# Later batches: K to lhs by DMA transposes, chunk bounds by a VectorE tree

## The chip, the cores and the metric

The kernel runs on one core of a Trainium2 chip. Its engines are TensorE (PE, matmuls; PEld is its weight load), VectorE (DVE), ScalarE (ACT), GpSimd (POOL) and SyncE (SP, which here only issues DMAs; ACT and POOL issue some as well). Each engine works through its own queue in order, and they wait for one another by semaphores. The metric is the device time of one execution in microseconds; the time of a kernel is the median of its runs. Less is better.

## What is computed

Attention in which every query attends to at most six chunks of 32 keys, then a two-layer MLP with an ELU. Batch 4, 8 heads, 768 positions, head dimension 64; the MLP goes from 512 to 2048 and back to 512 over all 3072 tokens.

```python
k_chunks = k.reshape(B, H, nc, chunk, D)                 # chunk = 32, nc = 24
k_min = np.min(k_chunks, axis=3)
k_max = np.max(k_chunks, axis=3)
ub = np.sum(np.maximum(q[:, :, :, None, :] * k_min[:, :, None, :, :],
                       q[:, :, :, None, :] * k_max[:, :, None, :, :]), axis=-1)
ub = np.where(pos[:, None] // chunk >= np.arange(nc)[None, :], ub, -1e9)
top_chunks = np.argsort(ub, axis=-1)[..., -6:]
scores = scale * np.matmul(q, k.transpose(0, 1, 3, 2))
mask = sel & (pos[:, None] >= pos[None, :])              # sel: key's chunk is among the query's six
attn = softmax(np.where(mask, scores, -1e9))
x = np.matmul(attn, v)                                   # heads side by side: 3072 x 512
h = x @ w_in
out = np.where(h > 0, h, np.exp(np.minimum(h, 0)) - 1) @ w_out
```

## The kernel before

**Tiling.** The work is cut into nine blocks of query positions: three of 256 in batch 0 (blocks 0 to 2) and two of 384 in each of batches 1 to 3 (blocks 3 to 8). Heads go in four pairs, so that a pair's two head dimensions fill 128 partitions. Per block there is a front (K and Q are brought into shape, chunks are selected), an attention part for each pair, and the MLP.

**Front.** K, Q and V come in as f32 tiles of 128 positions by 8 heads by 64 (`kld`, `qld`, `vld`, issued at L442). `prep_k` turns one pair's K with PE transposes against an f32 identity (L484, one per 128 positions, into PSUM). From that PSUM tile VectorE takes the maximum and the minimum of every 32 columns with two `tensor_reduce` (L504) and their difference (L521); minimum and difference are the weights `kst` of the bounds. ACT casts the same PSUM tile to bf16. In blocks 0 and 1 (`DIRECT_K`) it writes the two heads straight into `lhs` (L511); in the others it writes one tile `kb` (L516), and two DMAs per pair copy its halves to rows 0 to 63 of `lhs` (L519). Rows 64 to 95 of `lhs` hold a constant, -40000 where a key's chunk is the row's number, written once at the start (L418, and L420 by DMA for the second set). `prep_q` does the same for Q: PE transposes, ACT copies to `QTf` in f32 (L534), two casts per pair to rows 0 to 63 of `rhs` (by ACT in blocks 0 and 1, L538; by POOL in the others, L542), and a rectified copy `Qrl` on VectorE (L545).

**Selection.** The bounds are matmuls of `kst` with `QTf` and `Qrl` (L563). VectorE transposes them in 32 x 32 blocks (L574), finds the sixth largest of each query (L581), compares (L585) and transposes the 0/1 rows back, straight into rows 64 to 95 of `rhs` in blocks 0 to 2 (L591), or into `msk` (L597), from which eight DMAs copy them (L601). So a score matmul over 96 rows (L625) adds -40000 where a chunk isn't selected.

**Attention and MLP.** ACT takes the exponential of the scores into `pt` (L641, L645), VectorE zeroes what lies above the diagonal (L652, L659), PE multiplies with V, which has a column of ones (L674; `vext`, cast by POOL at L475), VectorE divides (L683, L685), and the result is turned into `xt` by a DMA transpose on SP (L698), or on PE in the first and last block. The MLP computes 16 groups of four matmuls per block (L713), each followed by an exponential on ACT (L717), a subtraction of 1 on POOL (L719) and the gate product `gT` on VectorE (L721, 144 in the kernel), and then the second layer (L732), whose result goes out over ACT (L736) and SP (L739). The f32 weights are loaded and cast by DMAs that POOL issues (L459, L463).

**Order.** Nothing is scheduled by hand line by line. Every step is an `op` with an engine, an assumed duration, its reads and writes, and a priority: the block's slot, plus a value per kind of step, block and engine from the table `SHIFTS`. `Plan.run` plays the steps through with these durations and so fixes each engine's order when the kernel is built; on the chip each engine follows it. `CAPS` gives the number of buffers per kind. PE's gaps up to an assumed 70 us are filled with matmuls on a junk tile (L849).

Of the kernel before, what the change touches and what calls it, by code (L numbers as in the profile page):

```python
# [48 lines left out]
DIRECT_K = (0,1)  # L49
# [3 lines left out]
MASK_DVE = (0,1,2)  # L53
SW_LOADS = ("k1","q1","v0","v1","k2","q2","v2")
ACT_LOADS = ("k0", "q0")
SW_ORDER = ("k1","v0","q1","v1","wi0","wi1","wi2","wi3","k2","q2","v2","wo0","wo1","wo2","wo3")
QC_ACT = (0, 1)
VC_ACT = ()
# [5 lines left out]
CAPS = dict(psT=1, psS=2, psO=1, psM=4, kld=2, qld=2, vld=1, QTf=6, Qrl=6, kb=3, kmx=3, ubT=2, thr=2,  # L64
# [8 lines left out]
    ('cast', 'POOL'): (23.69201, -1.09103, 8.72813, 12.08469, 27.05452, 15.31053, -7.22527, 12.46238, -4.92564),  # L73
    ('gate', 'POOL'): (-15.60205, 0.0, 0.0, 0.0, 0.0, 0.0, 0.0, 0.0, 0.0),
    ('init', 'DVE'): (2.32119, 0.0, 0.0, 4.74909, 8.35134, 25.74829, 26.2034, 24.17884, 8.09583),
    ('init', 'POOL'): (-10.70374, 13.48214, 0.0, 0.0, 0.0, 0.0, 0.0, 0.0, 0.0),
    ('init', 'SP'): (0.0, 0.0, 5.0031, 0.0, 0.0, 0.0, 0.0, 0.0, 0.0),
    ('kld', 'ACT'): (7.73677, 0.0, 0.0, 0.0, 0.0, 0.0, 0.0, 0.0, 0.0),
    ('kld', 'SP'): (10.12848, 0.0, 0.0, 5.57881, -2.49779, -2.11959, 2.10101, -9.36615, 8.45298),
    ('kld', 'POOL'): (0.0, -10.22887, -28.22296, 0.0, 0.0, 0.0, 0.0, 0.0, 0.0),  # L80
    ('mlp_in', 'ACT'): (-5.95241, -10.04818, -17.00783, -25.26762, -14.11138, -10.95442, -15.33449, -28.79886, -25.74958),
    ('mlp_in', 'DVE'): (-17.75866, -10.06772, 0.30993, -42.84851, -12.09763, -12.58286, -21.31407, -27.98266, -20.97106),
    ('mlp_in', 'PE'): (16.73975, -0.43165, -16.68227, -9.61, 1.47816, -3.63864, -12.99075, 8.98426, -6.01021),
    ('mlp_in', 'POOL'): (14.0813, -3.42504, -7.07691, 9.34007, -3.88006, 14.95892, 2.46731, -3.39101, -20.64038),
    ('mlp_out', 'ACT'): (4.22, -1.17489, -2.72673, 1.20556, 3.98277, -5.60986, 4.9958, 11.5461, -16.3697),
    ('mlp_out', 'PE'): (21.15925, 11.91005, 16.97289, -0.35066, 1.28499, 10.01749, 2.87573, 19.97835, -0.98046),
    ('mlp_out', 'SP'): (1.98487, -6.20708, 4.90006, 5.76266, -7.76736, -15.54093, 15.2713, 2.49768, -7.95696),
    ('prep_k', 'ACT'): (-19.18919, -30.78931, -27.5262, -6.91647, -6.7488, -6.36581, -3.55271, -15.77301, -8.33444),
    ('prep_k', 'DVE'): (-28.28537, -41.41256, -18.41797, -26.42048, 4.76573, -40.62348, -18.36229, -14.34176, -9.12351),
    ('prep_k', 'PE'): (-12.63275, 2.81869, -6.61429, -24.32332, 11.32822, -0.45579, -0.25696, 3.77564, -5.23277),  # L90
    ('prep_k', 'SP'): (0.0, 0.0, -13.31443, -2.45234, -6.22613, 4.3603, -1.19146, 4.6153, 18.19868),
    ('prep_q', 'ACT'): (-33.9716, -32.60888, -11.98557, -31.52365, -6.14348, -38.53006, -19.34522, -0.18424, -32.21482),
    ('prep_q', 'DVE'): (-12.55718, -8.37218, -7.36189, -0.77956, -17.2022, -13.25357, -2.48719, 12.39928, 9.4983),
    ('prep_q', 'PE'): (-0.49879, -10.22351, -6.76805, -3.36762, 13.26419, -0.11343, -0.82527, 2.63172, 17.99147),
    ('prep_q', 'POOL'): (0.0, 0.0, -1.80424, 5.83533, 31.22304, -2.13268, 13.63839, 14.88967, 8.56983),
    ('qld', 'ACT'): (4.95999, 0.0, 0.0, 0.0, 0.0, 0.0, 0.0, 0.0, 0.0),
    ('qld', 'SP'): (1.83573, 0.0, 0.0, 15.2204, -34.93755, -8.03456, -21.48739, -7.26273, -2.89049),
    ('qld', 'POOL'): (0.0, 18.35032, 4.84342, 0.0, 0.0, 0.0, 0.0, 0.0, 0.0),
    ('score', 'ACT'): (-15.06279, 15.94173, -8.66685, 9.77749, -9.24225, 2.15661, -0.32595, 11.29037, -1.82453),
    ('score', 'DVE'): (-14.86996, -1.8364, -14.54096, -15.51319, -24.21821, -11.17075, -7.10068, 12.60874, -21.25837),  # L100
    ('score', 'PE'): (-32.41584, -3.52461, -7.04682, -18.09124, -31.88096, -7.62331, -8.80699, -3.45233, -3.08179),
    ('select', 'DVE'): (15.81252, 43.76081, 24.59488, 29.28494, 4.04565, 23.13038, 28.69119, 20.70793, 39.51627),
    ('select', 'PE'): (-27.57642, 1.02863, -33.96822, -11.24403, -50.42777, -17.9141, -33.86792, -39.9782, -44.24463),
    ('select', 'SP'): (0.0, 0.0, 0.0, -13.94033, -23.5977, -19.02693, 6.4407, -14.63791, -5.86023),
    ('vld', 'POOL'): (-4.26654, 3.53215, -20.45399, 0.0, 0.0, 0.0, 0.0, 0.0, 0.0),
    ('vld', 'SP'): (0.0, 0.0, 0.0, 11.82217, -6.42843, 0.45266, 3.43084, -5.00112, 20.242),
    ('w_in', 'POOL'): (-5.96518, 0.0, 0.0, 0.0, 0.0, 0.0, 0.0, 0.0, 0.0),
# [202 lines left out]
def kernel(  # L310
# [68 lines left out]
    def pool_op(occ, fn, writes=(), reads=()):  # L379
        return op("POOL", occ, 60, fn, reads=reads, writes=writes)  # L380
# [500 lines left out]
```

## Time and profile before

| | us |
|---|---|
| median of three runs | 296.47 (296.07 to 300.57) |
| the profiled execution's own time | 297.83 |
| its span, first to last instruction | 295.9 |
| PE, DVE, ACT, POOL busy | 277.3, 204.8, 196.4, 137.0 |
| mean granted TensorE clock | 0.965 |

The span is what the views below divide up; it is 1.9 us shorter than the execution's own time. An engine is busy while at least one of its instructions runs. Instructions of one engine overlap somewhat (the next starts while the last one drains), so a group's mean duration is more than the distance at which such instructions follow one another; for PE, which is pipelined, much more.

```profile
L719 POOL TENSOR_SCALAR e<-e 128x384 f32<-128x384 f32 (+1 forms) x144 | 69.8, 489 | 120.6 <-ACT e L717 60.0
L721 DVE SCALAR_TENSOR_TENSOR gT<-psM,e 128x384 bf16<-128x384 f32 (+1 forms) x144 | 71.8, 506 | 25.4 <-POOL e L719 24.0
L516 ACT ACTIVATE kb<-psT 128x384 bf16<-128x384 f32 (+1 forms) x28 | 13.7, 489 | 12.0 <-DVE kst L504 7.8
L504 DVE TENSOR_REDUCE kmx<-psT 128x12 f32<-128x384 f32 (+1 forms) x32 | 16.6, 519 | 6.7 <-PE psT L484 6.3
L475 POOL TENSOR_SCALAR vext<-vld 128x384 bf16<-128x384 f32 (+1 forms) x36 | 17.5, 509 | 5.7 <-DMA vld<-in_v_dram 3.0
...
lhs<-kb SPq DMA_DIRECT2D x48, 48.0 KB, 2.6
...
xt<-on SPq DMA_TRANSPOSE x28, 2.8
```

These are groups of the page's fifth and sixth part: line, engine, operation, output and inputs, count, busy time in us and mean ns of one, then the engine's idle time just before them and who ended most of it; for DMA issues, count, size and median us from issue to landing.

### The profile page before, as it was taken

The numbers are of one execution on the slowest core, as the hardware profiler recorded it, in microseconds if no ns is written. First come the engines' busy times: TensorE is split into PE (matmuls) and PEld (weight loads), VectorE is DVE, ScalarE is ACT, GpSimd is POOL, SyncE is SP. The second block draws the span as 40 slices with busy tenths as digits, with TensorE's granted clock in tenths as the row PEclk, the third lists the DMA queues.
The fourth block names the chain that finished last, engine by engine and source line by source line (L and its number), as shares of the span: only waits on it lengthen the run. The fifth ranks groups of instructions, "written<-read, shape, count | busy, mean of one in ns | idle before, by whom it ended". The sixth has DMA issues, their size and how long they took to land.

```text
span 295.9 us, 7293 instructions
## 1 busy us (share of the span) xinstructions
PE 277.3 (94%) x2544; PEld 179.4 (61%) x2544; DVE 204.8 (69%) x667; ACT 196.4 (66%) x458; POOL 137.0 (46%) x278
## 2 busy tenths in 40 slices
PE   8576879999999998999999999999999999999993
PEld 8354557569658655666565556766565456655541
DVE  8778698897768886855699966666678727634620
ACT  2795587299559528997397349995496389854621
POOL 7697674034915924845365414750285024404510
PEclk9865798999999999999999999999999999999999
DMA  8889998268936665968845662602210420010001
GB/s 189 221 149 214 273 198 149 65 174 180 208 66 180 150 135 122 243 158 205 199 95 153 144 175 68 153 16 85 74 44 17 82 94 2 0 39 35 38 35 72
DMA packets 86885, 36.23 MB, mean 122 GB/s; under 512 B 74176, under 2 KB 82880, under 8 KB 86848
## 3 DMA queue, kind: packets, MB, share of 16 engines
q1 hardware_dynamic: 79424, 27.38, 37.7%
q0 software_dynamic: 5344, 7.87, 13.0%
q10 hardware_dynamic: 2080, 0.52, 0.8%
q8 instruction: 20, 0.33, 0.5%
q14 instruction: 17, 0.14, 0.2%
HBM read 27.26 MB, written 6.29 MB: 113 GB/s over the span
## 4 chain that ended last, share of the span: by engine, by line
PE 73%; DVE 13%; ACT 6%; DMA 4%; issue 2%; POOL 1%; SPq 0%; POOLq 0%; DVEq 0%; ACTq 0%
PE psM L713 23%; PE psM L732 23%; PE psS L625 10%; PE o_bank L674 6%; PE psT L484 5%; DVE gT L721 3%; PE psT L563 2%; DMA rhs<-msk 2%; PE o_bank L849 2%; ACT rhs L538 2%; DVE rhs L591 2%; DVE kmx L504 2%; ACT lhs L511 1%; DMA kld<-in_k_dram 1%; DVE thr L581 1%
## 5 line engine op out<-in xcount | busy, mean ns | idle before, releaser
L719 POOL TENSOR_SCALAR e<-e 128x384 f32<-128x384 f32 (+1 forms) x144 | 69.8, 489 | 120.6 <-ACT e L717 60.0
L713 PE MATMUL psM<-xt,w_in_sb 128*128 128x384 bf16 (+1 forms) x576 | 109.0, 313 | 1.6 <-DVE gT L721 1.4
L732 PE MATMUL psM<-w_out_sb,gT 128*128 128x512 bf16 x384 | 99.1, 379 | 0.0
L641 ACT ACTIVATE pt<-psS 128x384 bf16<-128x384 f32 (+1 forms) x164 | 87.7, 568 | 13.2 <-PE psS L625 12.7
L721 DVE SCALAR_TENSOR_TENSOR gT<-psM,e 128x384 bf16<-128x384 f32 (+1 forms) x144 | 71.8, 506 | 25.4 <-POOL e L719 24.0
L717 ACT ACTIVATE e<-psM 128x384 f32<-128x384 f32 (+1 forms) x144 | 68.8, 486 | 21.9 <-PE psM L713 18.4
L713 PEld LDWEIGHTS <-w_in_sb 128*128 128x128 bf16 x576 | 55.4, 99 | 28.1 <-issue 2.4
L625 PE MATMUL psS<-rhs,lhs 96*128 96x384 bf16 (+2 forms) x304 | 66.3, 286 | 2.5 <-DMA rhs<-msk 1.5
L732 PEld LDWEIGHTS <-gT 128*128 128x128 bf16 x384 | 36.0, 98 | 31.5 <-issue 1.2
L625 PEld LDWEIGHTS <-lhs 96*128 96x128 bf16 x312 | 29.4, 100 | 19.4 <-issue 2.3
L542 POOL TENSOR_SCALAR rhs<-QTf 64x384 bf16<-64x384 f32 (+1 forms) x56 | 29.4, 526 | 14.4 <-ACT QTf L534 10.8
L736 ACT ACTIVATE osb<-psM 128x512 f32<-128x512 f32 x24 | 14.4, 600 | 30.5 <-PE psM L732 30.3
L674 PEld LDWEIGHTS <-pt 128*128 128x128 bf16 x672 | 27.8, 99 | 9.8 <-issue 1.7
L674 PE MATMUL o_bank<-vext,pt 128*128 128x65 bf16 x672 | 30.9, 195 | 0.8 <-DVE on L685 0.5
L652 DVE TENSOR_TENSOR pt<-pt,tri 128x512 bf16<-128x512 bf16 x36 | 17.0, 475 | 7.0 <-ACT pt L641 6.6
L516 ACT ACTIVATE kb<-psT 128x384 bf16<-128x384 f32 (+1 forms) x28 | 13.7, 489 | 12.0 <-DVE kst L504 7.8
L504 DVE TENSOR_REDUCE kmx<-psT 128x12 f32<-128x384 f32 (+1 forms) x32 | 16.6, 519 | 6.7 <-PE psT L484 6.3
L534 ACT ACTIVATE QTf<-psT 128x384 f32<-128x384 f32 (+1 forms) x32 | 15.9, 498 | 7.6 <-PE psT L484 7.6
L475 POOL TENSOR_SCALAR vext<-vld 128x384 bf16<-128x384 f32 (+1 forms) x36 | 17.5, 509 | 5.7 <-DMA vld<-in_v_dram 3.0
L685 DVE TENSOR_TENSOR on<-o_bank,rcp 128x384 bf16<-128x384 f32 (+1 forms) x36 | 18.2, 506 | 0.6
L484 PE MATMUL psT<-ident_f,kld 128*128 128x128 f32 x88 | 16.0, 285 | 1.3 <-ACT QTf L534 0.6
L484 PE MATMUL psT<-ident_f,qld 128*128 128x128 f32 x88 | 15.8, 285 | 1.4 <-ACT lhs L511 1.0
(69 smaller groups left out, 241.6 us busy)
## 6 DMA issues: line engine op xcount, KB each, us to landing
out_dram<-osb SPq DMA_DIRECT2D x24, 256.0 KB, 2.2
kld<-in_k_dram SPq DMA_DIRECT2D x19, 256.0 KB, 4.0
qld<-in_q_dram SPq DMA_DIRECT2D x19, 256.0 KB, 3.9
vld<-in_v_dram SPq DMA_DIRECT2D x18, 256.0 KB, 3.5
lhs<-kb SPq DMA_DIRECT2D x48, 48.0 KB, 2.6
w_in_sb<-in_moe_w_in_dram POOLq DMA_DIRECT2D x4, 512.0 KB, 9.5
w_out_sb<-in_moe_w_out_dram POOLq DMA_DIRECT2D x4, 512.0 KB, 11.9
vld<-in_v_dram POOLq DMA_DIRECT2D x6, 256.0 KB, 5.0
```

What stands on the lines that cost most here:

```text
L484: nc.tensor.transpose(ps.get()[:, P * n:P * (n + 1)], xb.get()[:, n, hs, :].rearrange("p h d -> p (h d)"), ident_f)
L504: nc.vector.tensor_reduce(out=out, in_=psk.get()[:, 0:w].rearrange("p (c w) -> p c w", w=CHUNK), axis=AX.X, op=o)
L542: pool_op(110 + pool_ns(w), lambda h=h: nc.gpsimd.tensor_scalar(out=rhs[RH[i]][0:64, h, j, 0:w], in0=qtf.get()[64 * h:64 * h + 64, 0:w], s ...
L625: nc.tensor.matmul(sps.get()[:, o + pc:o + pc + n], lhsT=lhs[s][0:96, hd, P * kb:P * (kb + 1)], rhs=rhs[y][0:96, hd, j, c0 - lo:c0 - lo + ...
L641: op("ACT", act_ns(wtot), 140, lambda pt=pt, sps=sps, hd=hd, wtot=wtot: nc.scalar.activation(out=pt.get()[:, hd, 0:wtot], in_=sps.get()[:, ...
L674: nc.tensor.matmul(o3.get()[:, hd, qi, :], lhsT=pt.get()[:, hd, P * qt + off:P * qt + off + P], rhs=vexts[s][:, kb, hd, :], start=(kb == 0 ...
L685: op("DVE", dve_ns(w), 140, lambda: nc.vector.tensor_tensor(out=on.get()[:, 0:nt, :, :].rearrange("p q h d -> p h q d"), in0=o3.get()[:, : ...
L713: op("PE", 1 + w / 2.4, 200, lambda fc=fc, kk=kk, h_ps=h_ps: nc.tensor.matmul(h_ps.get()[:, 0:w], lhsT=w_in_sb[:, kk, P * fc:P * (fc + 1)] ...
L717: op("ACT", act_ns(w), 200, lambda e=e, h_ps=h_ps: nc.scalar.activation(out=e.get()[:, 0:w], in_=h_ps.get()[:, 0:w], func=AF.Exp), reads=[ ...
L719: op("POOL", pool_ns(w), 72, lambda e=e: nc.gpsimd.tensor_scalar(out=e.get()[:, 0:w], in0=e.get()[:, 0:w], scalar1=-1.0, scalar2=1.0, op0= ...
L721: g_ops.append(op("DVE", dve_ns(w), 130, lambda e=e, h_ps=h_ps, fc=fc: nc.vector.scalar_tensor_tensor(out=gT[fc // 4].get()[:, fc % 4, 0:w ...
L732: op("PE", 216, 200, lambda tt=tt, fc=fc, o_ps=o_ps: nc.tensor.matmul(o_ps.get(), lhsT=gT[fc // 4].get()[:, fc % 4, P * tt:P * (tt + 1)], ...
```

## The change

Batch 0 (blocks 0 to 2) keeps the PE transposes of K and the reduces. For batches 1 to 3 `prep_k` is no longer called. Three new steps take its place. `load_kn` lets POOL issue DMAs that load K as bf16 into tiles `kn`, 128 positions by 8 heads by 128, of which the second 64 columns of each head are padding that holds the constant of rows 64 to 95 (filled once by `init_pads` and `init_kn`). `turn_k` issues on SP one DMA transpose per tile, which writes all eight heads' `lhs` columns of these 128 positions, constant rows included. `bounds_k`, once per batch, loads K a second time in f32, chunk by chunk: a partition is one chunk of one head (96 partitions for four heads), and the 32 positions lie along the row. VectorE halves the row pairwise with `tensor_tensor` maximum and minimum, 1024, 512, 256, 128 and 64 elements, twice (for four heads each); two PE transposes per batch and four small ACT copies put the results into `kst`.

The Q casts of blocks 0 and 1 move from ACT to VectorE (`QC`). Block 2's K goes to `lhs` directly instead of over `kb`. `kb` and the DMA copies from it are gone, as are those of the constant rows. `lhs` becomes two tensors by batch parity, `rhs` two instead of three; Q and V are buffered tile by tile, and a V cast takes all eight heads of 128 positions. The order of POOL's first DMAs, some assumed durations and all of `SHIFTS` are new, so every engine's order is another.

```diff
-DIRECT_K = (0,1)
-QC_ACT = (0, 1)
+QC = {0: "DVE", 1: "DVE"}
-SW_ORDER = ("k1","v0","q1","v1","wi0","wi1","wi2","wi3","k2","q2","v2","wo0","wo1","wo2","wo3")
+SW_ORDER = ("k1", "q1", "v0", "v1", "wi0", "wi1", "wi2", "wi3", "k2", "q2", "v2", "wo0", "wo1", "wo2", "wo3")
...
+    def init_pads():
+        def go():
+            nc.vector.memset(pads, 0.0)
+            for x in range(4):
+                nc.vector.memset(pads[:, :, :].rearrange("p t r -> p (t r)")[32 * x:32 * x + 32, x:5 * 68 + x + 1:68], MASKNEG)
+
+    def init_kn(t):
+        pool_op(600, lambda: nc.gpsimd.tensor_copy(
+            out=kns[t][:, :, D:P], in_=pads[:, t:t + 1, :].to_broadcast([P, H, D])), [r_kn[t]], [r_pads])
...
+    def load_kn(i):
+        for t in range(lo // P, hi // P):
+            op("POOL", 940, (770, 159, 1000), lambda t=t: nc.gpsimd.dma_start(
+                out=kns[t][:, :, 0:D], in_=k[b, :, P * t:P * (t + 1)].rearrange("h p d -> p h d")), writes=[r_kn[t]])
+
+    def turn_k(i):
+        for t in range(lo // P, hi // P):
+            op("SP", 1400, (64 * dma_ns(256), dma_ns(256), -300), lambda t=t: nc.sync.dma_start_transpose(
+                out=lhs[b % 2][:, :, P * t:P * (t + 1)], in_=kns[t][:, :, :].rearrange("p h r -> p (h r)")),
+                reads=[r_kn[t]], writes=[r_lhs[b % 2][t]])
+
+    def bounds_k(i):
+        part = buf("kpart", [P, 2, 2, D], F32)
+        rows, half = 4 * NCH, CHUNK // 2 * D
+        for g in range(2):
+            cks = [buf("kld", [P, half], F32) for _ in range(2)]
+            top = buf("ktop", [P, half], F32)
+            for z in range(2):
+                o = op("SP", 640, dma(6, 4096), lambda g=g, z=z, cks=cks: nc.sync.dma_start(
+                    out=cks[z].get()[0:rows], in_=k[b, 4 * g:4 * g + 4].rearrange(
+                        "h (c z t) d -> z (h c) (t d)", z=2, t=CHUNK // 2)[z]),
...
+            for w, how, dst in ((1, AOT.max, top), (0, AOT.min, cks[0])):
+                def level(n, how=how, dst=dst):
+                    nc.vector.tensor_tensor(out=dst.get()[0:rows, 0:n], in0=dst.get()[0:rows, 0:n],
+                                            in1=dst.get()[0:rows, n:2 * n], op=how)
...
+                op("DVE", 1140, 115, lambda cks=cks, how=how, dst=dst: nc.vector.tensor_tensor(
+                    out=dst.get()[0:rows], in0=cks[0].get()[0:rows], in1=cks[1].get()[0:rows], op=how),
+                    reads=[*rs, *cks], writes=[dst])
...
-        if i in DIRECT_K:
-            for h in range(2):
-                op("ACT", 60 + act_ns(w), 90, lambda h=h: nc.scalar.activation(
-                    out=lhs[s][0:64, h, lo:hi], in_=psk.get()[64 * h:64 * h + 64, 0:w], func=AF.Copy),
-                    reads=[psk], writes=[r_lhs[s][x]])
-        else:
-            kb = buf("kb", [P, QMAX], BF16)
...
+        for h in range(2):
+            op("ACT", 60 + act_ns(w), 90, lambda h=h: nc.scalar.activation(
+                out=lhs[0][0:64, 2 * j + h, lo:hi], in_=psk.get()[64 * h:64 * h + 64, 0:w], func=AF.Copy),
+                reads=[psk], writes=[r_lhs[0][t] for t in range(lo // P, hi // P)])
...
+            if how == "DVE":
+                op("DVE", 90 + 0.47 * w, 110, lambda src=src, dst=dst: nc.vector.tensor_copy(out=dst(), in_=src()),
+                   reads=[qtf], writes=r_out)
+                continue
...
     def load_kq(i):
-        load(ldk, k, i, "kld", at)
+        if BLOCKS[i][0] == 0:
+            load(ldk, k, i, "kld", at)
+        else:
+            load_kn(i)
+            if BLOCKS[i][1] == 0:
+                bounds_k(i)
         load(ldq, q, i, "qld", at)
...
         for j in range(NPAIR):
-            prep_k(j, i)
+            if BLOCKS[i][0] == 0:
+                prep_k(j, i)
             prep_q(j, i)
+        if BLOCKS[i][0]:
+            turn_k(i)
         select(i)
```

## The prediction

> **What bounds the kernel now.** First the page's busy shares and slices. TensorE (PE) is busy 94%, but a PE counted busy is not a PE at its peak, so I looked at where it loses time.
>
> ```profile
> PE 277.3 (94%) x2544; PEld 179.4 (61%) x2544; DVE 204.8 (69%) x667; ACT 196.4 (66%) x458; POOL 137.0 (46%) x278
> ...
> PE   8576879999999998999999999999999999999993
> ...
> DVE  8778698897768886855699966666678727634620
> ```
>
> VectorE (DVE) is full in the first third and in slices 20 to 22, and has room at the end. Second, PE's timeline in a full stretch gives what each matmul really holds: start to start.
>
> ```profile
> 115.80 1.14 PE L713 MATMUL psM<-xt,w_in_sb 128*128 128x384 bf16 x6
> 116.77 0.33 PE L625 MATMUL psS<-rhs,lhs 96*128 96x384 bf16 x1
> ...
> 121.41 0.49 PE L484 MATMUL psT<-ident_f,kld 128*128 128x128 f32 x3
> 121.73 0.33 PE L625 MATMUL psS<-rhs,lhs 96*128 96x384 bf16 x1
> ```
>
> Six 384-column matmuls take 0.97 us (0.162 each); three K transposes 0.32 (0.109 each, not the 0.285 that the group row gives as a mean). In the same way 0.216 for 512 columns, 0.109 for 256, 0.055 for 128, 0.030 for a 65-column one of L674, and 0.81 us (192 queries) to 1.45 (384) for a bounds step. Times the counts this is 254.5 us of PE work in a span of 295.9: 41.4 are lost. Third, the gate products (L721, 144 in the kernel) as mileposts, their times from the timeline, and the busy times of the stretches between them:
>
> ```profile
> 0.00:30.60 30.60, 21.82 (x218) 17.34 (x219) 23.02 (x81) 18.78 (x51) 22.77 (x48) 0.77 0.93 198
> 30.60:63.90 33.30, 30.72 (x301) 21.10 (x300) 28.76 (x108) 21.45 (x54) 14.24 (x33) 0.91 0.80 161
> 63.90:94.60 30.70, 29.93 (x337) 22.93 (x336) 23.09 (x82) 24.13 (x62) 16.09 (x36) 1.00 0.69 166
> 94.60:185.90 91.30, 89.34 (x807) 55.78 (x805) 69.65 (x224) 62.59 (x145) 46.30 (x91) 1.00 0.64 156
> 185.90:282.10 96.20, 96.19 (x854) 58.23 (x851) 59.74 (x174) 67.62 (x149) 37.51 (x73) 1.00 0.18 49
> ```
>
> (Columns after the length: PE, weight load, DVE, ACT, POOL busy; clock; DMA share; GB/s.) The ends are the 1st, 17th, 41st, 89th and last gate product. PE work queued up to each is 6.7, 30.6, 60.3, 147.9, 244.0 us, so the time lost is 23.9, 33.3, 34.3, 38.0, 38.1, and 41.4 at the end. Up to the 17th, DVE and ACT set the pace (DVE 51.8 busy of 63.9); afterwards PE does, losing 8.1 in 232 us.
>
> **The change, part by part.** *PE.* Batches 1 to 3 lose 72 K transposes: 72 x 0.109 = 7.9 us. Six transposes of 96 columns come in, at 0.085 (below the 128-column row) 0.5. PE work falls to 247.1. After 63.9 us this is worth its length as long as PE stays the bound.
>
> *DVE, removed.* 48 reduces of 384 columns. Back to back they start 0.47 apart (the row's 0.55 contains overlap), so 22.6 us, and 24 small subtracts at about 0.13, 3.1.
> *DVE, added.* Three pairwise trees. No 1024-element instruction with both operands in SBUF is in this trace; reduces of 256 and 384 columns, 0.34 and 0.47 apart, give 0.075 us plus 1.02 ns an element. A tree step of 1024, 512, 256, 128, 64 elements then costs 1.12 + 0.60 + 0.34 + 0.21 + 0.14 = 2.4 us, four per batch with the subtract 9.8, in all 29.4. Its upper bound is what POOL can do to such an instruction: the causal mask (L652) takes 0.43 or 0.74, the latter while POOL runs casts, a factor of 1.7.
>
> ```profile
> 158.49 0.74 DVE L652 TENSOR_TENSOR pt<-pt,tri 128x512 bf16<-128x512 bf16 x1
> ...
> 161.18 0.43 DVE L652 TENSOR_TENSOR pt<-pt,tri 128x512 bf16<-128x512 bf16 x1
> ```
>
> I take the uncontended value, which is the commoner (median 0.426 of 36). [...]
> The 16 Q casts of batch 0's first two blocks go from ACT to DVE: nearest rows L545 (0.34 for 128x256) and L696 (0.29); 0.3 each, 4.8 (ends 0.2 and 0.5). A memset of mask rows and the pads, 1.3.
>
> *DVE by milepost.* The built order of the changed program puts all three trees ahead of the 89th gate product, the first ahead of the 41st, and also moves the selection for block 4 ahead of the 41st (4.6 us by its rows: two bound transposes, 24 maxima at 0.08, two compares, two mask transposes) with four Q rectifications and two small steps (2.3). Up to the 41st: +4.8 +9.8 +1.3 +4.6 +2.3 -16 x 0.47 -7 x 0.13 = +14.3, so 89.2 busy instead of 74.9. Up to the 89th: about +18, 162.7. PE work ahead of the same points is 61.8 and 144.2. Between them DVE has 73.5 against PE's 82.4: hidden. Up to the 41st it has 89.2 against 61.8, in a stretch that DVE already paced, and this is where the saving is spent.
>
> *ACT* loses 24 casts kb (L516), 12.1 us, and the 16 casts L538, 6.6; it gains eight half-height K casts for block 2 in place of four full ones (3.0 - 1.6) and twelve small copies of bounds (at most 0.38 each as L534, I take 0.25). L538 holds 6.1 us of the chain of the first 62; what is late next there is DVE, which receives that work. Elsewhere ACT was hidden, so nothing is gained.
>
> *POOL* gains 18 DMA issues for K (L442 row, 0.94: 17 us) and six pad copies (0.6 by the V casts: 3.7), loses 2.6 as 36 V casts become 24 wider ones. Cover: POOL is 46% busy. Behind each issue wait the e steps that gate products need (L721 waited 24.0 us on L719), so at worst 17, at best 0; I take 0 after the 41st, since PE lost only 7 us there with such waits present. At the start the pads and four K tiles stand ahead of w_in: its first DMA, issued at 16.55 and landed 6.8 later, is first used at 28.64, slack 5.2; its issue moves by 3.7 + 4 x 0.94 = 7.5, so 0 to 2.3 us.
>
> *SP and DMA.* 56 copies kb to lhs (0.58 each, 32 us) and four mask-row copies leave; 18 transposes of eight 128x128 blocks come. The nearest row is the transpose to xt of two or three blocks: 1.2 us to issue, 2.8 to landing. Ends: 1.2 and 8.4 us (by blocks); I take near the low one, because two and three blocks issue alike. Each waits for its K tile to land and its lhs to be free; behind it on SP stand xt, mask copies and loads.
> [...]
> The small edits have one answer: loads buffered tile by tile, two rhs buffers for three and the Q transposes held behind the block's earlier bounds step only move waits that the order already contains; new priorities likewise. They cost nothing by themselves, and 1 us of PE's loss if a buffer comes late, well inside the ends below.
> In return the order leaves more PE work between a block's bounds and its first scores (11, 12, 9, 24, 16 us for blocks 4 to 8; 7, 7, 15, 6, 9 before), which covers the mask copies that held the chain for 3.7 and 3.35 us. I count at most 2 us for it, in the range only.
>
> **The sum.** The 41st gate product comes after 89.2 us of DVE work plus DVE's idle time. That idle time was 19.7 before, 12.1 of it up to the 17th, with ACT as a partner that is now lighter. Ends: 4 (DVE nearly never waits; PE's own path, 61.8 + 34.3 = 96.1 less at most 3 for the shorter ACT chain, allows no less than 93) and 19.7 as before. I take 10, between DVE's share in its fullest stretches (4.5 idle of 33.3) and the start's 7.6 of 30.6: 99.2 us instead of 94.6. From there PE work of 185.3 plus the 7.1 lost there before: 192.4. Span 291.6 (ends 285.4 and 301.3). The profiled execution took 297.83, 1.9 more than its span, and 1.36 above the median of the three runs; so 291.6 + 1.9 - 1.4 = 292.1, ends 286 and 302. A difference under 2% (below 290.5 or above 302.4) counts as no change here.
>
> **Rivals.** *DVE finds room and PE keeps all it saves* (0.33): the 41st at 96.1, span 288.5, time 289.0, down to 285.5. For it: PE lost 1 us between the 17th and the 41st; against it: DVE was 86% busy up to the 17th.
> *POOL slows the trees* (0.12; the other side): at 1.7 times, each batch's tree takes 16.7. The first adds 6.9 on the path; the other two put 87.2 of DVE work beside 82.4 of PE, some 5 more. Span 303.5, time 304. It decides once a 1024-element step averages above 1.7 us. Against it: most L652 are at 0.43; for it: POOL gets 18 us more work.
> *Long transposes delay xt* (0.07): at 8.4 us each, two ahead of an xt make 17 against 5.6 us of PE work between weighing and its MLP; at two such places half of 11 each, plus 11 with the forecast: 303. Against it: xt's issue doesn't grow with blocks.
> *The removed transposes weren't on the path* (0.03): PE's loss absorbs them, 296 to 297. Against it: PE is back to back after 63.9.
> The forecast, 0.45, covers 289 to 298, a quarter of it below 290.5. So faster 0.33 + 0.10 = 0.43, slower 0.12 + 0.05 = 0.17, within 0.40. Range 285.5 to 302.
>
> **What would show it.** PE transposes of K down to 24 and PE work near 247; the 41st gate product at 97 to 102 us; DVE busy near 213, with first tree steps of 1.1 to 1.3 us and 1.9 if POOL interferes; K transposes landing in about 3 us, and no wait of scores or MLP on them; after the 41st, losses of about 7 us. A later first gate product than 33 us, PE waits on lhs or xt, or gate products waiting for POOL behind K issues would make it wrong.

## The result and the profile after

The changed kernel takes 322.41 us (median of four runs, 321.0 to 326.5) against 296.27 of the kernel before on the same chip: a ratio of 1.088, 95% interval 1.082 to 1.094. It is slower, and outside the range. Some executions of a kernel run a per cent or two longer (300.57 before, 326.5 after), and the ratios leave these out. The profiled execution took 323.29 us, its span is 321.6.

The lines of the changed kernel's page that answer to those of before, with its DMA slices:

```profile
PE 277.2 (86%) x2477; PEld 173.3 (54%) x2477; DVE 224.7 (70%) x681; ACT 190.4 (59%) x434; POOL 162.2 (50%) x290
...
PE   7374985866969699978998889899999999999995
...
DVE  8879696479898298869789989585866503764420
...
DMA  6699999999969949999797599602033011000011
```

PE is now below 9 for most of the first half, and DMA stands at 9 in most slices up to the 25th, some 200 us. Next the stretches between the same mileposts, the gate products (L823 now), with the columns as before:

```profile
0.00:35.10 35.10, 20.89 (x210) 16.33 (x211) 29.55 (x102) 12.89 (x33) 28.56 (x52) 0.73 1.15 154
35.10:71.10 36.00, 26.82 (x252) 18.11 (x258) 24.80 (x79) 19.01 (x48) 20.11 (x38) 0.93 1.60 192
71.10:122.40 51.30, 42.57 (x443) 28.68 (x427) 40.42 (x149) 32.32 (x76) 30.03 (x54) 0.90 1.11 144
122.40:216.10 93.70, 85.46 (x760) 51.51 (x759) 78.28 (x217) 61.57 (x139) 51.64 (x89) 1.00 0.90 171
216.10:308.40 92.30, 92.30 (x794) 54.72 (x791) 51.12 (x138) 62.81 (x138) 31.86 (x61) 1.00 0.13 39
```

The DMA share is the summed time of all packets over that of 16 engines, so above 1 packets overlap; it was 0.93, 0.80, 0.69, 0.64 and 0.18 before. The last column was 198, 161, 166, 156 and 49 GB/s: far more packet time, but no more bytes a second (161 GB/s up to the 41st gate product, 175 before). The damage is over at the 89th gate product: behind it PE works without a gap, as before. Time lost (a milepost less the PE work queued up to it, the prediction's own measure), for both kernels and for four experiments below:

| lost up to, us | 1st | 17th | 41st | 89th | end |
|---|---|---|---|---|---|
| before | 23.9 | 33.3 | 34.3 | 38.0 | 41.4 |
| before, K for nothing (e10) | 23.3 | 31.1 | 33.1 | 35.5 | 38.7 |
| new order, K and bounds for nothing (e7) | 24.9 | 35.9 | 44.2 | 45.7 | 48.0 |
| new order, bounds, no K by DMA (e3) | 25.7 | 36.5 | 46.5 | 54.9 | 57.1 |
| new order, K by DMA, no bounds (e12) | 27.9 | 45.3 | 60.8 | 62.3 | 64.4 |
| after | 28.4 | 44.9 | 60.6 | 71.9 | 74.5 |

PE's work fell from 254.5 to 247.1 us as forecast; the loss rose by 33.1, of which 26.3 stand ahead of the 41st gate product.

The chain of waits of the changed kernel shows the first of them (start, length, what ended the wait):

```profile
4.93 4.75 POOL kn L441 x6
...
14.46 7.26 DMA vld<-in_v_dram
...
26.86 22.77 DMA lhs<-kn
...
50.16 0.09 POOL kn L492
...
59.53 6.93 DMA kld<-in_k_dram
```

The six pad copies hold POOL for 4.75 us while no first-block load has been issued on it; a K transpose issued at 26.86 lands 22.77 us later, and what the chain has waiting for it is not PE but POOL, with the next K load (L492) that refills a tile; a load for the tree, at 59.53, takes 6.93. What SP did meanwhile is in its timeline:

```profile
13.81 23.75 SPq L499 DMA_TRANSPOSE lhs<-kn  x4
37.65 6.68 SPq L517 DMA_DIRECT2D kld<-in_k_dram  x1
48.14 10.99 SPq L800 DMA_TRANSPOSE xt<-on  x3
```

The first four K transposes take SP from 13.8 to 37.6, 22.1 us of it in two waits for K tiles to land. The first line below is this wait (total, times, longest); the second the time from issue to landing of all 18 transposes (the first four took 6.6 to 23.7 us, the other fourteen 3.1 to 7.3):

```profile
SPq L499 <- DMA kn<-in_k_dram: 22.1, 2, 11.8
...
DMA to landing us min/median/max: 3.1/5.2/23.7
```

And the DMA queues (packets, MB, share of 16 engines): the software queue, which carries what POOL issues, had 5344 packets before, 7.87 MB and 13.0%.

```profile
q0 software_dynamic: 24064, 10.23, 34.4%
```

The 18 K loads of 1024 rows bring 18,720 more packets, 1040 each. K also comes in a second time for the tree: 31.98 MB read instead of 27.26.

### The profile page after: what moved, and what is told of

The parts are those of the page before. It is cut to its first block, busy times and chain, and to the rows that moved or that the text cites. A ratio compares the mean times of both kernels' runs of the same rounds, so it can differ in the third digit from the quotient of the medians.

```text
span 321.6 us, 7070 instructions
## 1 busy us (share of the span) xinstructions
PE 277.2 (86%) x2477; PEld 173.3 (54%) x2477; DVE 224.7 (70%) x681; ACT 190.4 (59%) x434; POOL 162.2 (50%) x290
## 3 DMA queue, kind: packets, MB, share of 16 engines
q0 software_dynamic: 24064, 10.23, 34.4%
q10 hardware_dynamic: 2080, 0.52, 0.9%
HBM read 31.98 MB, written 6.29 MB: 119 GB/s over the span
## 4 chain that ended last, share of the span: by engine, by line
PE 49%; DVE 21%; DMA 20%; POOL 4%; issue 3%; ACT 2%; SPq 0%; ACTq 0%; DVEq 0%; POOLq 0%
PE psM L815 18%; PE psM L834 17%; DMA lhs<-kn 7%; PE psS L727 7%; DMA kld<-in_k_dram 7%; DMA vld<-in_v_dram 4%; PE o_bank L776 4%; DVE kld L525 3%; DVE gT L823 3%; DVE ktop L525 2%; DVE kld L534 2%; DMA rhs<-msk 2%; DVE Qrl L646 2%; PE psT L664 2%; DVE ktop L534 2%
## 5 line engine op out<-in xcount | busy, mean ns | idle before, releaser
L821 POOL TENSOR_SCALAR e<-e 128x384 f32<-128x384 f32 (+1 forms) x144 | 72.8, 510 | 107.7 <-ACT e L819 92.4
L815 PE MATMUL psM<-xt,w_in_sb 128*128 128x384 bf16 (+1 forms) x576 | 112.0, 316 | 10.8 <-DVE gT L823 7.9
L834 PE MATMUL psM<-w_out_sb,gT 128*128 128x512 bf16 x384 | 101.5, 380 | 0.0
L743 ACT ACTIVATE pt<-psS 128x384 bf16<-128x384 f32 (+1 forms) x164 | 85.2, 554 | 22.8 <-PE psS L727 21.1
L823 DVE SCALAR_TENSOR_TENSOR gT<-psM,e 128x384 bf16<-128x384 f32 (+1 forms) x144 | 70.7, 504 | 31.9 <-POOL e L821 31.2
L819 ACT ACTIVATE e<-psM 128x384 f32<-128x384 f32 (+1 forms) x144 | 66.3, 471 | 38.7 <-PE psM L815 37.3
L643 POOL TENSOR_SCALAR rhs<-QTf 64x384 bf16<-64x384 f32 (+1 forms) x56 | 31.7, 566 | 19.7 <-ACT QTf L623 9.4
L776 PEld LDWEIGHTS <-pt 128*128 128x128 bf16 x672 | 27.9, 99 | 12.3 <-issue 3.0
L646 DVE TENSOR_SCALAR Qrl<-QTf 128x192 f32<-128x192 f32 (+3 forms) x36 | 18.0, 504 | 6.3 <-ACT QTf L623 6.1
L492 POOL DMA_DIRECT2D kn<-in_k_dram x18 | 16.4, 913 | 10.9 <-DMA lhs<-kn 6.3
L572 POOL TENSOR_SCALAR vext<-vld 128x512 bf16<-128x512 f32 x24 | 16.9, 718 | 4.6 <-DMA vld<-in_v_dram 4.5
L785 DVE RECIPROCAL rcp<-o_bank 128x6 f32<-128x6 f32 (+1 forms) x36 | 6.6, 184 | 16.0 <-PE o_bank L776 15.7
```

What stands on the lines that cost most here:

```text
L572: op("POOL", pool_ns(512), 60, lambda n=n: nc.gpsimd.tensor_scalar(out=vext[:, NPAIR * (b % 2):NPAIR * (b % 2) + NPAIR, lo // P + n, :, 0: ...
L643: pool_op(110 + pool_ns(w), lambda h=h: nc.gpsimd.tensor_scalar(out=rhs[RH[i]][0:64, h, j, 0:w], in0=qtf.get()[64 * h:64 * h + 64, 0:w], s ...
L646: op("DVE", 90 + 0.47 * (w - q0), 120, lambda: nc.vector.tensor_scalar(out=qrl.get()[:, q0:w], in0=qtf.get()[:, q0:w], scalar1=0.0, scalar ...
L743: op("ACT", act_ns(wtot), 140, lambda pt=pt, sps=sps, hd=hd, wtot=wtot: nc.scalar.activation(out=pt.get()[:, hd, 0:wtot], in_=sps.get()[:, ...
L776: nc.tensor.matmul(o3.get()[:, hd, qi, :], lhsT=pt.get()[:, hd, P * qt + off:P * qt + off + P], rhs=vext[:, s, kb, hd, :], start=(kb == 0) ...
L815: op("PE", 1 + w / 2.4, 200, lambda fc=fc, kk=kk, h_ps=h_ps: nc.tensor.matmul(h_ps.get()[:, 0:w], lhsT=w_in_sb[:, kk, P * fc:P * (fc + 1)] ...
```

## The experiments

Theories before the first runs. D: DMA is saturated by the K loads, the transposes and the second K, everything lands late, and queues that work in order (POOL, SP, VectorE behind a load) pass it on to PE. V: the work moved to VectorE (trees, Q casts) makes it the bound early. Two more were formed on the way: C, both, one behind the other, and O, the new order itself, with all that the small edits changed (buffer numbers too). The experiments leave every engine's order of the changed kernel as it is and drop or alter steps when they are emitted, except where said. Times below are ratios times 296.0 us, by which the changed kernel has 322.0; the texts of what was expected use medians.

**e1, K not awaited.**

```diff
-                out=lhs[b % 2][:, :, P * t:P * (t + 1)], in_=kns[t]...
+                out=lhs[1][:, :, P * t:P * (t + 1)], in_=kns[t]...
-                nc.tensor.matmul(..., lhsT=lhs[b % 2][0:96, 2 * j + hd, P * kb:P * (kb + 1)],
+                nc.tensor.matmul(..., lhsT=lhs[0][0:96, 2 * j + hd, P * kb:P * (kb + 1)],
```

> All scores read the K of batch 0 (scores of batches 1 to 3 use the wrong K); the 18 transposes still run, all into the other K buffer, in the same places. So all DMA traffic and the queues of SP and POOL stay, and PE no longer waits for K itself. Theory D (DMA and in-order queues): the late landings reach PE mostly through SP and POOL, on which other work is queued, so only a few us come back: 312 to 320 us against 322.4 of the changed kernel. Theory V (VectorE is the bound early): nothing comes back, 320 to 323. If PE's wait for K were the cause by itself: 300 to 305.

Measured 1.086 (1.080 to 1.093), 321.5 us: nothing comes back, as V has it. PE's wait for K itself costs nothing that can be measured. This misses D's 312 to 320; what D needs must come from removing traffic.

**e2, no transposes; e3, no K path at all.** To the second edit of e1, steps left out at emission:

```diff
         for o in plan.order:
...
+            if o.key[0] and o.key[0][0] in ['turn_k']:                    # e2
+            if o.key[0] and (o.key[0][0] in ['turn_k', 'kn'] or o.key[0] in [('init', 4), ('init', 5)]):   # e3
+                continue
             o.fn()
```

> As the run before (scores read batch 0's K), and the 18 DMA transposes of K are left out; the 18 K loads, the pads and the trees stay. Theory D: SP is freed of the waits of up to 22 us on K's landings and DMA of 18 transposes; the bound loads and masks leave on time: 302 to 312 us. Theory V: 318 to 323, since DVE's work is the same.

> As the run before, and the 18 K loads with their pad copies on POOL and the memsets of the pads are left out too: no K comes by DMA, while the trees, their loads and the Q casts stay on VectorE. Theory D: nearly all of the 33 us of extra loss goes, 290 to 300 us, software DMA packets fall from 24,064 to some 5,600, and the first gate product comes at about 31 us. Theory V: at least 312 us, since DVE keeps 39 us of tree and 7 us of casts.

Measured 1.073 (1.067 to 1.079) and 1.034 (1.029 to 1.038): 317.5 and 305.9 us. The transposes are worth 4.0 us (e1 to e2, give or take 2.6 by the intervals), loads and pads 11.6. V alone falls, and so does "nearly all" of D: e2 stays short of its 302 to 312, and with no K by DMA 10 us over the kernel before remain. e3's chain names DMA with 1% (20% after) and VectorE with 26%.

**e4, a short tree; e6, the same without the K path.**

```diff
-                    for n in (4 * D, 2 * D):
-                        level(n)
-                op("DVE", 600, 115, lambda level=level: level(8 * D), ...
+                op("DVE", 600, 115, lambda level=level: None, ...
```

> The tree steps of 512, 256 and 128 elements are left out (wrong chunk bounds for batches 1 to 3); the steps of 1024 and 64 elements and every load stay, so DVE has 12 x about 1.45 us = 17 to 18 us less work. Theory V: 12 to 18 us come back, 304 to 310 us. Theory D: only the chain's own trees get shorter, 3 to 6 us, 316 to 320.

> No K by DMA as in the run that measured 306.1 us, and the tree steps of 512, 256 and 128 elements left out too (wrong bounds and scores for batches 1 to 3), which takes some 17 us of DVE's work. Theory C (two causes one behind the other: DMA sets the pace first, and once it is gone the trees on VectorE do): 292 to 298 us, 8 to 14 less than with whole trees, where the same cut gave 1.2 us beside the DMA path. Theory O (the new order itself, or its loads, holds the rest): 303 to 306.

e4 measured 1.075 (1.065 to 1.084), 318.1 us; e6 1.009 (1.005 to 1.012), 298.6. The same cut of VectorE work is worth 3.9 us beside the K path (1 to 7 by the intervals) and 7.3 without it. So the tree costs too. That it does so partly behind DMA, as theory C has it, is only hinted at: e6 is just above C's 292 to 298, and e12 below speaks against it.

**e7, K and bounds for nothing.** e3 with one kind of step more left out:

```diff
-            if o.key[0] and (o.key[0][0] in ['turn_k', 'kn'] or ...
+            if o.key[0] and (o.key[0][0] in ['turn_k', 'kn', 'bounds_k'] or ...
```

> No K by DMA, and the whole bounds step of batches 1 to 3 left out: its 12 loads of 384 KB, the trees, the PE transposes and the ACT copies (the selection of these batches then works on old or zero bounds). Theory C: 286 to 294 us, the floor that this order has with K for nothing. Theory O: 300 us or more.

Measured 1.000 (0.996 to 1.004), 296.1 us. Neither range: the bounds step is worth 9.8 us, and yet this kernel, which no longer spends anything on K in three batches out of four, is only as fast as the one before.

**e10, the old order with K for nothing.** The kernel before, without `kld` and `prep_k` of blocks 3 to 8 and without the second set of constant rows:

```diff
-                nc.tensor.matmul(..., lhsT=lhs[s][0:96, hd, P * kb:P * (kb + 1)],
+                nc.tensor.matmul(..., lhsT=lhs[j][0:96, hd, P * kb:P * (kb + 1)],
...
+            if o.key[0] and (o.key[0][0] in ['kld', 'prep_k'] and o.key[0][1] > 2 or o.key[0] == ('init', 2)):
+                continue
```

> The kernel before, in its own order, with K for nothing in batches 1 to 3: their K loads, K transposes, reduces, K casts and K copies are left out (scores read batch 0's K, the selection works on old or zero bounds). It stands against the run of the new order with K and bounds for nothing, which took 295.95 us. Theory O (the new order loses by itself what is left): 282 to 290 us, since PE has the same work as there. If both orders have the same floor: 294 to 297 us.

Measured 0.975 (0.969 to 0.982), 288.7 us. The old order gives PE's saving nearly in full, 7.3 us (it is 7.9 of work); the new one, with the same PE work, loses 7.4. Theory O has its share. The windows of e10 and then of e7 show where:

```profile
31.00:62.00 31.00, 27.11 (x285) 18.32 (x285) 25.80 (x101) 19.74 (x49) 13.88 (x31) 0.98 0.70 144
62.00:84.00 22.00, 21.87 (x257) 15.94 (x259) 13.22 (x51) 15.32 (x40) 12.05 (x27) 1.00 0.50 114
```

```profile
31.00:62.00 31.00, 26.65 (x236) 18.48 (x237) 20.42 (x73) 18.20 (x48) 14.15 (x29) 0.86 0.72 119
62.00:84.00 22.00, 18.20 (x173) 13.11 (x173) 15.38 (x51) 16.97 (x40) 12.74 (x28) 0.92 0.79 157
```

From 62 to 84 us PE in e7 is idle for 3.8 of 22 us, and the granted clock is 0.92 there and 0.86 before that, against 1.00 and 0.98 in e10 (ahead of 31 us both are lower, 0.75 and 0.69). By the pages' slices the clock of e7 stands at 7, 8 and 8 tenths from 36.8 to 58.9 us and at 7 from 66.3 to 73.7, that of e10 at 9 everywhere behind 35.7. What a lower clock does to a matmul is in the trace of the changed kernel: from 54.99 us, at 0.50, six of 256 columns take 1.28 us (0.21 each); from 47.02, at 1.00, three take 0.33 (0.11). So by estimate up to 5.5 us of the loss come as a lower clock: 0.14 x 31 + 0.08 x 22 = 6.1, less e10's 0.02 x 31 = 0.6, if PE were busy throughout. No engine is full there. The new order puts block 3's Q preparation between block 2's scores, and VectorE waits for ScalarE:

```profile
DVE Qrl L646 <- ACT QTf L623: 5.8, 5, 1.7
```

(Waits of e7 between 60 and 86 us: in total, times, longest.)

**e15, that preparation later.** From e7, steps sorted by start, with those of blocks 3 and 4 5 us later and what depends on them behind:

```diff
+    late = {("prep_q", 3), ("select", 3), ("prep_q", 4), ("select", 4)}
+    for o in plan.order:
+        when[o] = max([o.start + (5000 if o.key[0] in late else 0)] + [when[d] + 1 for d in o.deps])
+    plan.order.sort(key=lambda o: when[o])
```

> The new order with K and bounds of the later batches for nothing (295.95 us, against 287.67 of the old order with K for nothing), with the Q preparation and the selection of blocks 3 and 4 put 5 us later in every queue, with all that depends on them. If putting these steps between the scores of block 2 is what holds the new order back between 62 and 84 us: 290 to 293.5 us. If the loss lies in the rest of the order: 295 to 299 us.

Measured 1.044 (1.039 to 1.050), 309.1 us: 13 us worse, where 3 to 6 better or no change were expected. Its 33rd gate product comes at 99.9 us (98.9 in e7), the 41st at 113.8 instead of 105.7. So that reading of the wait is not the cure: which steps of the new order cost the 7.4 us stays open. Nor was order parted from buffers: e7 also has two `rhs` for three and five `QTf` and `Qrl` for six.

**e8, small K loads; e13, the same bytes in wide rows.** Both from e2.

```diff
-                out=kns[t][:, :, 0:D], in_=k[b, :, P * t:P * (t + 1)].rearrange("h p d -> p h d")
+                out=kns[t][:, 0:1, 0:D], in_=k[b, 0:1, P * t:P * (t + 1)].rearrange("h p d -> p h d")      # e8
+                out=kns[t][:, 0:4, :]..., in_=k[b]...[8 * P * t:8 * P * (t + 1)].rearrange("(p e) d -> p (e d)", e=8)   # e13
```

> As the run without the 18 transposes (317.6 us; scores read batch 0's K), but each of the 18 K loads brings only one of its eight heads: 128 rows instead of 1024. The issues on POOL, their order and the pads stay, seven eighths of the small packets go. If the packets on the DMA engines cost the 11.5 us between that run and the one with no K path: 306 to 310 us. If POOL's queue and the pads ahead of the first loads do: 314 to 318 us.

> As the run without the 18 transposes (317.6 us; scores read batch 0's K), with K loads of the same bytes in 128 rows of 2 KB each instead of 1024 rows of 256 bytes (other K elements, unused). With an eighth of rows and bytes it was 310.1 us. If the number of small packets is what costs: 309 to 312 us. If the bytes do: 315 to 318 us.

e8 measured 1.048 (1.042 to 1.054), 310.3 us; e13 1.053 (1.049 to 1.058), 311.8. Seven eighths of the loads' traffic are worth 7.1 us, and 5.7 of these come back with all the bytes kept, in fewer and longer packets. The queue of e13, which carries as many MB as that of e2 (24064 packets, 32.6%):

```profile
q0 software_dynamic: 7936, 10.23, 18.8%
```

**e9, K by DMA for batch 3 only.** Pads and trees stay.

```diff
-                nc.tensor.matmul(..., lhsT=lhs[b % 2][0:96, 2 * j + hd, P * kb:P * (kb + 1)],
+                nc.tensor.matmul(..., lhsT=lhs[b // 3][0:96, 2 * j + hd, P * kb:P * (kb + 1)],
...
+            if o.key[0] and o.key[0][0] in ['kn', 'turn_k'] and o.key[0][1] < 7:
+                continue
```

> The K loads and transposes of batches 1 and 2 are left out (their scores read batch 0's K); batch 3 gets its K by DMA as changed, pads and trees stay. Theory D in its sharper form (the path costs only where the DMA engines are already full, up to about 200 us): 306 to 310 us, at most 3 more than with no K path, and that from the pads at the start. If each K tile costs the same wherever it comes: 311 to 312 us.

Measured 1.050 (1.045 to 1.056), 310.8 us, between the two ranges. Its first gate product is at 35.1 us (32.4 in e3), its 17th at 66.0 (62.7), its 41st at 112.4 (108.3), although no K load is issued before 95.8 us. So some 3 to 4 of the 4.9 us above e3 come from the pads (one profiled execution each, so to a us or so). The path itself in batch 3 then costs about 1 us, as the sharper D has it; the transposes land in 3.2 to 6.9 us there, against up to 23.7.

**e16, early K later.** The changed kernel, whole, sorted as in e15:

```diff
+    late = {("init", 5), ("kn", 3), ("kn", 4), ("kn", 5), ("kn", 6), ("turn_k", 3), ("turn_k", 4)}
+        when[o] = max([o.start + (20000 if o.key[0] in late and o.start < 65e3 else 0)] + [when[d] + 1 for d in o.deps])
```

> The changed kernel, whole, with the pads and the K loads and K transposes of batch 1 and the K reloads of batch 2 that stand ahead of 65 us put 20 us later in the queues of POOL and SP, behind the loads of w_in and the first V. Theory D by place (what costs is that K's packets stand ahead of the first blocks' loads): first gate product at 32 to 33 us and 313 to 318 us in all. If the packets cost the same later, since the DMA engines stay full until 200 us: 320 to 325 us.

Measured 1.098 (1.091 to 1.105), 325.0 us. The first gate product comes 1.5 us earlier, at 33.6, and the gain is lost by the 33rd (119.3 against 115.2). Put 20 us later, the traffic costs no less.

**e5 and e11, the Q casts.** In e5 the changed kernel casts on ScalarE; in e11 the kernel before casts on VectorE.

```diff
-                ... lambda src=src, dst=dst: nc.vector.tensor_copy(out=dst(), in_=src()),            # e5
+                ... lambda src=src, dst=dst: nc.scalar.activation(out=dst(), in_=src(), func=AF.Copy),
-                op("ACT", ..., lambda h=h: nc.scalar.activation(out=rhs..., in_=qtf..., func=AF.Copy),  # e11
+                op("ACT", ..., lambda h=h: nc.vector.tensor_copy(out=rhs..., in_=qtf...),
```

> The same part undone: the changed kernel with the 16 Q casts on ScalarE, in the place where VectorE had them. Theory V for the start: 316 to 320 us against 322.4. If DMA covers it there: 321 to 324 us.

> One part of the change alone: the kernel before, with the 16 Q casts of the first two blocks on VectorE in the place where ScalarE had them. Theory V for the start (VectorE paces it, each 0.44 us of cast on it is late): 299 to 303 us. The forecast's view (a shorter chain of ScalarE makes up for it): 294 to 298 us.

e5: 1.090 (1.084 to 1.095), 322.5 us, no change. e11: 1.004 (1.001 to 1.007), 297.2 us: some 1.2 us of cost (0.1 to 2.2 by the interval), although its first gate product moves from 30.6 to 33.3. e17 puts the casts back on ScalarE in e7, where no DMA covers them:

> The new order with K and bounds of the later batches for nothing (295.95 us), with the 16 Q casts back on ScalarE. Beside the DMA path this gave 0.5 us. If the casts are part of the 8.3 us by which the new order's floor is above the old one's, hidden until now by DMA: 291 to 294 us. If not: 295 to 297 us.

Measured 1.005 (1.002 to 1.008), 297.5 us, if anything slower. The casts aren't the order's loss.

**e12, no bounds; e14, trees without loads; e18, the first bounds step only.** From the changed kernel: e12 leaves out `bounds_k`, e18 only for blocks 5 and 7 (batches 2 and 3); e14 keeps the steps, without the loads:

```diff
+            if o.key[0] and o.key[0][0] == 'bounds_k':                        # e12
+            if o.key[0] in [('bounds_k', 5), ('bounds_k', 7)]:                # e18
+                continue
...
-                o = op("SP", 640, dma(6, 4096), lambda g=g, z=z, cks=cks: nc.sync.dma_start(...)
+                o = op("SP", 640, dma(6, 4096), lambda: None,
-                    in0=cks[0].get()[0:rows], in1=cks[1].get()[0:rows], op=how),
+                    in0=zt[0:rows].to_broadcast([rows, 4, 256]), in1=zt[0:rows].to_broadcast([rows, 4, 256]), op=how),
```

> The changed kernel with its K loads and DMA transposes, but without the bounds step of batches 1 to 3: 12 loads of 384 KB, the trees, the PE transposes and ACT copies (the selection works on old or zero bounds). Theory C (DMA first, the trees behind it): 316 to 321 us; the loads that leave free some of the crowded DMA engines. If the two causes simply add: 311 to 313 us.

> The changed kernel with the whole K path by DMA and whole trees on VectorE, but without the 12 loads of 384 KB that feed the trees: their first step reads a block of zeros (the bounds of batches 1 to 3 are zero). Loads and trees together were worth 11.1 us (311.3 us without both). If VectorE waits for late loads and the trees themselves find room: 311 to 315 us. If the trees' work costs: 319 to 323 us.

> The changed kernel with the bounds step (loads, trees, PE transposes, ACT copies) for batch 1 only; batches 2 and 3 select on older bounds. All three steps together are worth 11.1 us. If the first is covered by the late DMA up to the 41st gate product and the two later ones cost all of it between the 41st and the 89th, where the forecast had VectorE hidden: 310 to 313 us. If each costs a third: 314 to 316.5 us.

e12 measured 1.052 (1.043 to 1.060), 311.3 us: 10.7 us beside the K path, 9.8 without it (e3 to e7), so the two causes add, and C falls. e14: 1.080 (1.074 to 1.087), 319.8, so the loads by themselves are worth 2.2 us, not clear of noise, and VectorE's work most of the rest (the six PE transposes and twelve ACT copies are in it). e18: 1.053 (1.044 to 1.061), 311.6, nearly e12: the two later steps cost, and the first next to nothing where DMA is late. The ratio rests on two runs, so this leans as much on the table above, where after and e12 lose the same up to the 41st and then 11.3 against 1.5. PE's waits between 122 and 206 us, in the changed kernel and then in e12:

```profile
PE psM L815 <- DVE gT L823: 2.7, 3, 1.0
PE psT L546 <- DVE kpart L539: 2.2, 2, 1.5
PE o_bank L776 <- DVE pt L761: 1.7, 1, 1.7
PE o_bank L776 <- DVE on L787: 1.6, 2, 1.2
```

```profile
PE psS L727 <- issue: 0.2, 1, 0.2
```

With the trees PE waits 8.2 us there for VectorE: 6.0 for small steps and 2.2 for the bounds themselves (`kpart`). Without, no wait for VectorE is left. VectorE's timeline of the changed kernel shows tree steps back to back, and then a place where small steps are queued behind one:

```profile
130.36 1.22 DVE L534 TENSOR_TENSOR ktop<-kld 96x1024 f32<-96x1024 f32 x1 [0.85 <-DMA kld<-in_k_dram]
131.62 1.22 DVE L534 TENSOR_TENSOR kld<-kld 96x1024 f32<-96x1024 f32 x1
132.76 0.68 DVE L525 TENSOR_TENSOR ktop<-ktop 96x512 f32<-96x512 f32 x1
...
142.20 1.27 DVE L534 TENSOR_TENSOR ktop<-kld 96x1024 f32<-96x1024 f32 x1 [1.95 <-DMA kld<-in_k_dram]
143.40 0.58 DVE L761 TENSOR_TENSOR pt<-pt,tri 128x256 bf16<-128x256 bf16 x1
143.90 0.54 DVE L823 SCALAR_TENSOR_TENSOR gT<-psM,e 128x384 bf16<-128x384 f32 x1
144.37 0.67 DVE L525 TENSOR_TENSOR ktop<-ktop 96x512 f32<-96x512 f32 x1
144.97 0.54 DVE L823 SCALAR_TENSOR_TENSOR gT<-psM,e 128x384 bf16<-128x384 f32 x1
```

The mask step of 0.58 and the gate products stand behind a tree step that waited 1.95 us for its load and then worked 1.2. ScalarE had finished the mask step's input at 140.27 (L747), 3.1 us before VectorE came to it, and PE waited 1.7 us for the mask step.

**The whole.** In steps of one thing removed, of the time before: floor of the old order -2.5%, the new order +2.5%, the bounds step +3.3%, pads, K issues and an eighth of the loads +1.5% (e8 to e3), the other seven eighths +2.4% (e2 to e8), transposes +1.4% (e1 to e2), waiting for K itself +0.2% (after to e1): +8.8% in all. That it adds up is no test, since each run is the start of the next step; and each step is known to 0.6 to 0.9 points, so the last is not clear of nothing. All that K for nothing gains in the old order is 2.5%; and since the new order with K and bounds for nothing is no faster than the kernel before, no repair of the K path alone can make it so. No version came out of this that beats the kernel before.

## Why the prediction was wrong

- **PE work falls to 247:** right. K's PE transposes are 24 and the work is 247.1 us. That the saving is worth its length is right too, in the old order: 7.3 us (e10).
- **The tree's price, 2.4 us a chain:** about right. The steps of 1024 start some 1.2 us apart (130.36, 131.62, then 132.76; forecast 1.12), those of 512 0.60 apart (0.60); the page's sum of 40.1 us contains overlap: two rows of 512, each 0.68 long, start at 132.76 and 133.36. The rival of a POOL that slows trees was to hold above 1.7 us; the two rows of 1024 average 1.27 and 1.38, so it did not hold.
- **"Between them DVE has 73.5 against PE's 82.4: hidden":** this step failed for 10 us (e12, e18). The work measured there was 78.3 and 82.4 us, but sums of two engines' work say nothing of order: a tree step, and the load it waits for, stand in VectorE's queue ahead of small steps that PE needs. The slack of 8.9 us that was counted on, 4.1 as measured, was no cover.
- **"SP and DMA ... I take near the low one":** this step failed for 15 us together with the next one. DMA was priced by one transfer's landing as the trace of before had it, not by the load on the DMA engines. They were at 0.93, 0.80 and 0.69 up to the 41st gate product already, and got 18,720 more packets and the transposes: landings of eight blocks in 3.1, 5.2 and 23.7 us (least, median, most; forecast about 3). Of the 15.6 us the transposes made 4.0, and the loads that feed them 7.1 with seven eighths of their traffic.
- **POOL, "0 to 2.3" at the start, 0 later:** mis-sized. The first gate product came at 35.1 us instead of 30.6, and at 32.4 with the K path left out (e3), so 2.7 of it are the K path's. Only w_in was checked for slack; the 4.75 us of pads stand ahead of the first K, Q and V loads on POOL as well. Pads and issues, with an eighth of the loads, are 4.4 us (e3 to e8).
- **Idle time of VectorE up to the 41st, taken as 10, with 19.7 as the upper end:** 27.6 (122.4 less 94.8 busy; 89.2 were forecast). The model that VectorE's sum sets this milepost failed: with K and bounds for nothing it still comes at 105.7 (e7) instead of 90.8 (e10), and with the K path at 122.4. This is the largest error, 23 of 30 us, and made of the others.
- **"The order leaves more PE work ... at most 2 us":** wrong sign. I looked at the mask copies of blocks 4 to 8 only. The new order loses 7.4 us, all of it ahead of the 41st gate product by the table; which of its steps or buffers do it stays open, and up to 5.5 us of it, by estimate, come as a lower clock.
- **Q casts:** 0.44 us each by their row instead of 0.3, and worth some 1.2 us in the old order, nothing clear in the new.
- **Long transposes delay xt:** in part. `xt` landed in 12.3 us (median of three) in the first 60 us, 2.4 (of four) before. By the times K's loads weigh more than the transposes: 7.1 us for seven eighths of them (e2 to e8) against 4.0 (e1 to e2); for `xt` itself the two were not parted.

## What to carry to other kernels

Before moving work from an engine to DMA, read the DMA share of the very stretch where it will lie: here, at 0.7 to 0.9, new transfers made others land later (in the median `vld` from POOL 7.8 us instead of 5.0, `w_out` 16.0 instead of 11.9), and the count of their rows mattered more than their bytes (of 7.1 us, 5.7 came back with all the bytes in an eighth of the rows). Work that fits by sums into a slack engine can still cost when it stands in one queue ahead of small steps that the bound engine needs, 9.8 to 10.7 us here; look at what is queued behind each long or waiting instruction. To price a removal, make the removed work free in the old order and in the new one: here that showed a ceiling of 2.5% and an order that had already spent it.

## What the hardware showed unexpectedly

From queue shares, times spans, times 16: the 18,720 software packets that e2 has over e3 took (0.326 x 317.5 - 0.143 x 304.2) x 16 = 960 us of DMA engine time, 51 ns for a row of 256 bytes read and 128 written. That is no fixed price. In the changed kernel 2080 of these packets took 0.322 x 13 x 16 = 67 us from 117 to 130 us, 32 ns each, and as many 0.768 x 10 x 16 = 123 us from 136 to 146, 59 ns each; the DMA share was 0.83 and 1.72 there. Where it is above 1 packets overlap, so the higher prices are not those of a row alone. In e13, 2592 packets more than in e3 took 236 us, 91 ns for a row eight times as long: eight small rows cost 4.5 times one wide in the crowd, and 2.8 times at 32 ns. The 18 transposes took (0.430 x 321.6 - 0.334 x 317.5) x 16 = 516 us on the hardware queue (after less e2), about 29 us of engine time for eight blocks, or 1.8 us of all 16 engines; other packets of that queue that became slower are in this difference.

Last, the granted clock. Behind 47.1 us the kernel before keeps 1.00 up to its end, with PE 97% busy. The changed kernel falls to 0.50 three times there: from 53.7 to 57.1, 77.6 to 84.4 and 108.3 to 111.7 us. In the 7 us ahead of each, PE was busy for 61, 68 and 50%, and its longest wait was 1.5, 1.6 and 3.5 us; inside, it was busy for 86, 94 and 100%, so that the half clock falls on work: by estimate half of 12.7 busy us, 6.4, on top of the idle time. Yet from 57.1 to 70.6 us the clock stays at 1.00 with PE 72% busy and a wait of 2.5 us. What sets off a fall, no run here shows.
